# A linear-attention block with an MLP behind it: fewer, wider warming products and a new order of all instructions

## The chip, the cores and the metric

The kernel runs on one core of a Trainium2 chip. The metric is the device time of one execution in microseconds (us); lower is better. The engines are named as in the profile: PE (matrix products), PEld (its weight loads), DVE (vector), ACT (activations), POOL, SP (here it issues all DMAs).

## The reference

For x of 2048 rows and 512 columns (bf16):

```
ln(x)  = (x - mean) / sqrt(var + 1e-5)                  # by row
q,k,v  = split(ln(x) @ wqkv), 32 heads of 16
phi(t) = where(t > 0, t + 1, exp(t)) + 1e-6
kv     = sum_s phi(k)_s v_s^T      z = sum_s phi(k)_s   # by head
o      = (phi(q) kv) / (phi(q) z + 1e-6)
h      = x + o @ wo
out    = h + relu(ln(h) @ w1) @ w2                      # w1: 512 x 1792
```

## The kernel before

Rows come in 16 tiles of 128 (index t) or 4 chunks of 512 (index c). Every instruction is issued by hand: the string ORDER is a list of words such as `K.4.5`, and the last loop of the kernel calls the function of each word in turn. Each engine runs its own instructions in the order of the list, and waits on semaphores where data or a buffer is not ready yet. SP too runs its DMAs in order, and a DMA may not go out before the eighth DMA ahead of it has landed. The numbers behind a word are the tile or chunk, and often the bank of PSUM (0 to 7, the tile `bk`) that the products go to.

The words that the text speaks of, with the engine and the line of the profile before:

- `warm` (PE, L245): products of zeros with zeros, read by nobody, at the very start.
- `lx` (SP, L214), `lk`, `lq`, `lv`, `lo`, `l1`, `l2` (SP, L220): loads of x, of the three parts of wqkv, of wo, w1, w2.
- `S`, `A` (DVE, L248, L249), `R` (ACT, L254 and L255), `N` (DVE, L262): statistics, mean and variance, 1/sqrt, and the normalized tile, which is written to h_nat.
- `T` (PE, L287) and `E` (ACT, L297): the first five tiles are transposed by PE into lnT. `X` (SP, L308): the other eleven are transposed by DMA. `t`, `v`, `x` do the same for the second layer norm (`s`, `a`, `r`, `n`).
- `K` (PE, L316) and `Q` (PE, L324): products for k by tile and for q by chunk, four products of 512 columns each. `F`, `U` (ACT, L334, L337), `M`, `D` (DVE, L341, L344), and `qF` to `qD` for q: phi of them.
- `G` (PE, L368): sums phi(k)^T ln(x) over all tiles in four banks; `kv` (PE, L414) and `m` (PE, L426) bring wv and wo into one matrix m_sb. `z` (PE, L392) sums phi(k).
- `d4` (PE, L440), `dl4`, `dx4` (ACT, L446, L451): the denominators and, by logarithm and exponential, their inverse. `wb` (SP, L468) writes it to memory, eight `rb` (SP, L471) read it back spread over 16 rows each into rr, and `dm` (DVE, L484) multiplies.
- `h` (PE, L493), `hD` (DVE, L499): the attention output plus x.
- `p`, `ph` (PE, L508, L517), `pD`, `pA` (DVE, L528, ACT, L523): ln(h) @ w1 and relu. `f` (PE, L537), `fo` (DVE, L545), `fd` (SP, L552): product with w2, scale and add, and the store of a tile of the output. `f` goes in two halves of seven products.

The word of the warming is read as `warm.<count>.<bank>.<columns>`. A bank is shared by whoever comes next: a product that starts in it waits until the engine that read the last result is done.

Of the kernel before, what the change touches and what calls it, by code (L numbers as in the profile page):

```python
# [15 lines left out]


ORDER = """
table const masks warm.70.7.64 warm.2.7 lx.0.1 S.0 A.0 R.0.1 lx.1.1 S.1 lx.2.1 A.1 N.0 T.0.1 lk.0.4 S.2 R.1.1
N.1 T.1.2 lx.3.1 A.2 E.0 K.0.4 R.2.1 lx.4.2 S.3 N.2 T.2.1 E.1 A.3 S.5 R.3.1 K.1.0.0.2 K.1.0.2.2 N.3 S.4 A.5 A.4  # L20
E.2 T.3.2 K.2.6.0.2 K.2.6.2.2 F.0.1 M.0.1 lx.6.2 E.3 S.7 lq.0.4 R.4.2 lx.8.4 Q.0.3.1 N.4 U.0.1 A.7 F.1.1 F.2.1
T.4.2 N.5 S.6 Q.0.1.4 U.1.1 M.1.1 A.6 lx.12.4 M.2.1 D.0.1 R.6.2 K.3.7.0.2 K.3.7.2.2 E.4 X.5 U.2.1 U.3.1 D.1.1
N.6 Q.0.0.3 N.7 S.10 qF.0.0.2 K.4.5 K.5.6 S.8 A.10 S.9 A.8 qU.0.0.2 S.12 F.4.2 D.2.1 X.6 Q.0.2.0 A.9 A.12 K.6.2
S.13 S.11 M.4.2 A.11 A.13 U.4.2 D.4.2 F.3.1 R.8.2 N.9 M.3.1 X.7 K.7.3 R.12.2 R.10.2 N.8 F.6.2 D.3.1 N.13 S.15
G.0 G.1 U.6.2 S.14 X.9 X.8 N.10 A.14 A.15 N.12 qM.0.0.2 M.6.2 X.13 qF.0.2.2 R.14.2 qU.0.2.2 qM.0.2.2 N.11 G.2
G.3 G.5 G.4 N.14 X.12 K.9.3 K.8.2 K.13.1 N.15 qD.0.0.2 D.6.2 za.4.1 X.11 X.10 F.8.2 U.8.2 M.8.2 K.12.0 U.12.2
F.12.2 G.7 za.6.0 K.11.3 D.8.2 qD.0.2.2 M.12.2 za.8.0 K.10.2 F.10.2 X.14 G.8 K.14.0 U.10.2 X.15 K.15.1 M.10.2 zf
lv.2.2 lv.0.2 G.9 D.10.2 zhi D.12.2 F.14.2 G.6 G.10 G.11 M.14.2 zlo U.14.2 D.14.2 z.0.0 z.2.0 z.3.0 z.1.0 G.14
lo.0.2 lo.2.2 zc zh d4.0.1 dl4.0 l1.0.2 G.13 G.12 G.15 dx4.0 gA.2.2 Q.1.1.3 Q.1.0.2 qF.1.0.2 gD.0.2 kv.1.4
kv.3.4 kv.0.4 kv.2.4 kx qU.1.0.2 qM.1.0.2 qD.1.0.2 Q.1.3.1 Q.1.2.0 qF.1.2.2 m.0.2 m.1.3 mD.0.2 m.3.7 m.2.6 wb.0  # L30
Q.2.0.4 Q.2.1.5 rb.0.7 rb.0.1 rb.0.6 rb.0.3 rb.0.0 rb.0.2 rb.0.4 rb.0.5 l1.2.2 qM.1.2.2 qU.1.2.2 Q.2.3.1
qD.1.2.2 mA.2.2 qF.2.0.2 Q.2.2.0 qU.2.0.2 dm.0.2.2 dm.0.0.2 qM.2.0.2 h.1.6 hD.1 s.1 a.1 qU.2.2.2 d4.1.3 dl4.1
h.0.7 hD.0 s.0 dx4.1 h.2.6 h.3.5 a.0 l2.0.7 wb.1 hD.2 nA.1 hD.3 qF.2.2.2 nA.0 s.2 s.3 Q.3.0.2 Q.3.1.3 a.2
Q.3.3.6 a.3 qF.3.0.2 qU.3.0.2 Q.3.2.5 x.1 r.0.4 qF.3.2.2 n.2 t.2.7 n.3 t.3.4 qD.2.0.2 v.2 v.3 x.0 ph.0.3.1.0
ph.0.1.3.0 ph.0.2.0.0 ph.0.3.1.1 qM.2.2.2 qM.3.0.2 ph.0.0.2.0 ph.0.0.2.1 qM.3.2.2 qD.3.0.2 qU.3.2.2 qD.2.2.2
ph.0.2.0.1 qD.3.2.2 p.0.7.5 d4.2.6.2 pD.0.2.2 dl4.2 dl4.3 rb.1.4 rb.1.6 rb.1.3 rb.1.2 rb.1.0 rb.1.1 ph.0.1.3.1
rb.1.7 rb.1.5 p.0.6.4 dx4.2 dm.1.0.2 dm.1.2.2 h.4.0 pD.0.0.2 hD.4 pD.0.6.2 p.0.5.1 h.6.6 dx4.3 p.0.4.0 hD.6
l2.7.7 h.5.4 pA.0.4.2 s.4 s.6 hD.5 h.7.7 a.4 a.6 p.0.11.6 p.0.10.5 s.5 hD.7 a.5 p.0.9.4 wb.2 rb.2.6 n.4 rb.2.0
rb.2.4 s.7 n.6 rb.2.3 rb.2.2 rb.2.1 a.7 n.5 n.7 rb.2.5 rb.2.7 dm.2.0.2 dm.2.2.2 pD.0.10.2 p.0.13.1 p.0.12.0
p.0.8.3 pD.0.12.2 wb.3 r.4.4 rb.3.0 rb.3.4 h.10.7 hD.10 x.6 h.8.2 h.11.6 hD.8 s.10 rb.3.5 rb.3.1 rb.3.6  # L40
f.1.0.0.7 rb.3.3 rb.3.2 rb.3.7 s.8 hD.11 pD.0.8.2 h.9.5 f.3.1.0.7 x.7 x.5 s.11 a.8 hD.9 f.1.0.7.7 f.0.4.0.7 a.10
a.11 x.4 dm.3.2.2 dm.3.0.2 h.14.7 h.12.3 s.9 n.11 h.15.6 a.9 n.10 h.13.2 fo.1 n.9 n.8 hD.14 s.14 hD.12 x.11
hD.15 f.0.4.7.7 r.8.4 p.1.13.7 p.1.6.3 a.14 hD.13 s.12 s.15 s.13 a.12 a.15 a.13 n.14 p.1.12.6 n.13 f.3.1.7.7
n.12 n.15 p.1.2.5 fo.0 pD.1.12.2 x.10 p.1.7.4 fo.3 p.1.3.6 x.9 pD.1.6.2 pD.1.2.2 r.12.4 x.8 p.1.11.2 p.1.10.1
pD.1.10.2 f.2.4.0.7 p.2.0.6 p.2.1.7 f.2.4.7.7 pD.2.0.2 p.2.10.0 p.2.11.1 fo.2 x.14 p.2.6.2 p.2.7.3 x.15 fd.3
p.2.13.7 p.2.12.6 pD.2.10.2 pD.2.6.2 x.12 fd.1 pD.2.12.2 p.2.2.0 x.13 fd.0 p.2.3.1 p.1.5.6 p.1.4.5 pD.2.2.2
pD.1.4.2 p.1.0.3 p.1.1.4 p.1.9.1 p.1.8.0 pD.1.0.2 pD.1.8.2 f.4.4.0.7 f.4.4.7.7 fo.4 fd.4 f.5.3.0.7 f.5.3.7.7
fo.5 fd.2 f.6.7.0.7 f.6.7.7.7 fo.6 p.2.4.2 p.2.5.3 f.7.0.0.7 f.7.0.7.7 pD.2.4.2 fo.7 p.3.6.1 p.3.7.2 pD.3.6.2
p.3.8.3 p.3.9.4 p.3.5.1 pD.3.8.2 p.3.4.0 pD.3.4.2 fd.6 p.3.10.3 p.3.11.4 pD.3.10.2 p.3.2.0 p.3.3.1 p.3.0.5
p.3.1.6 pD.3.2.2 pD.3.0.2 p.3.13.3 fd.7 p.3.12.2 pD.3.12.2 f.10.1.0.7 f.15.2.0.14.3.1 f.15.7.0.14.0.2 p.2.8.4  # L50
p.2.9.5 fo.15.3.1 fd.15.3.1 fo.15.0.2 pD.2.8.2 f.8.7.0.7 f.10.1.7.7 fo.10 f.8.7.7.7 fo.8 f.14.2.0.7 f.14.2.7.7
f.13.3.0.7 fd.5 fd.8 fd.10 fo.14 f.13.3.7.7 fo.13 f.9.0.0.7 f.9.0.7.7 fd.15.0.2 f.11.6.0.7 f.11.6.7.7 fd.13 fo.9
f.12.0.0.7 fd.9 f.12.0.7.7 fo.11 fd.14 fd.11 fo.12 fd.12 f.15.2.0.14.2.1 fo.15.2.1 fd.15.2.1
"""


# [1 line left out]
def kernel(  # L58
# [14 lines left out]
    S, D = xf.shape  # L73
# [7 lines left out]
    KD = D // P  # L81
    KF = FF // P
# [5 lines left out]
    const = ctx.enter_context(tc.tile_pool(name="const", bufs=1))  # L88
# [58 lines left out]
    rb = big.tile([P, NE, 2, CW], BF16, name="rb")  # L147
# [10 lines left out]
    def pk(t, n=1):  # L158
        return pk_lo[:, t : t + n, :] if t < 2 else acts[0][:, t - 2 : t - 2 + n, :]
# [152 lines left out]
    def op_K(t, b, k=0, n=KD):  # L312
        c, j = divmod(t, CT)
        at_bank["k", t] = b
        for kd in range(k, k + n):
            nc.tensor.matmul(  # L316
                bk[:, b, :], lhsT=lnT[c][:, kd, j * P : (j + 1) * P], rhs=wk_sb[:, kd, :],
                start=(kd == 0), stop=(kd == KD - 1),
            )

    def op_Q(c, j, b):
# [211 lines left out]
    def op_f(t, b, f0, n, k=0, w=KD):  # L533
        c, j = divmod(t, CT)
        at_bank["f", t, k] = b
        for f in range(f0, f0 + n):
            nc.tensor.matmul(  # L537
                bk[:, b, 0 : w * P], lhsT=acts[c % 2][:, f, j * P : (j + 1) * P],
                rhs=w2_sb[:, f, k * P : (k + w) * P],
                start=(f == 0), stop=(f == KF - 1),  # L540
            )

    def op_fo(t, k=0, w=KD):
# [44 lines left out]
```

## Time and profile before

| what | value |
|---|---|
| median of 3 runs | 169.89 us (169.71 to 170.19) |
| span of the profiled execution | 168.0 us |
| between the span and the median | 1.9 us |
| PE busy | 162.7 us (97%) |
| DVE, ACT busy | 115.6 us (69%), 49.5 us (29%) |
| granted TensorE clock, mean | 1.000 |
| DMA | 16.01 MB, 25003 packets |

The span runs from the first to the last instruction of one profiled execution; the time of a run is longer by what lies around it, and no time of the profiled execution apart from its span is given. A row of the timeline begins with the start and the length in us, and "x4" says how many instructions are merged in it. The bracket at its end is the idle time of the engine ahead of it and what ended that. Rows of groups end with busy time, mean length in ns, and idle time before. In the DMA rows the last number is the median time from issue to landing.

### The profile page before, as it was taken

The page shows a single profiled execution, that of the slowest core. Times are in us where ns is not written, and L with a number is a line of the kernel's source. Part 1 is how long each engine was busy: PE and PEld are TensorE (multiplying, and loading weights), DVE is VectorE, ACT ScalarE, POOL GpSimd, SP SyncE. Part 2 cuts the span into 40 slices and gives each one's busy share as a digit, 9 for nine tenths or more (in the row PEclk, how much of TensorE's full clock was granted, in tenths as well). Part 3 has the DMA queues.
Part 4 walks back from the last instruction along what each step waited for, and adds up shares of the span by engine and source line. Part 5 has one row for each costly group of instructions (what it writes and reads, how often), then busy time and mean ns, then how long its engine had stood idle before and what let it go on. Part 6 is the DMA issues. An engine that isn't in the chain of part 4 may idle for free.

```text
span 168.0 us, 2417 instructions
## 1 busy us (share of the span) xinstructions
PE 162.7 (97%) x924; PEld 79.2 (47%) x924; DVE 115.6 (69%) x217; ACT 49.5 (29%) x83; POOL 4.8 (3%) x21
## 2 busy tenths in 40 slices
PE   7799999999999999999999999999999999999992
PEld 7444444454544754444444444444444447444442
DVE  3899999942579999999999755764144773432312
ACT  3799968715798843100101000000000000000000
POOL 7400000000000000000000000000000000000000
PEclk9999999999999999999999999999999999999999
DMA  4984054681595364414552520000101000011021
GB/s 108 353 298 88 20 106 95 189 301 45 132 337 161 98 205 132 132 48 123 83 102 57 126 63 0 0 0 0 62 31 35 0 0 7 32 34 48 31 94 39
DMA packets 25003, 16.01 MB, mean 95 GB/s; under 512 B 15008, under 2 KB 23968, under 8 KB 24992
## 3 DMA queue, kind: packets, MB, share of 16 engines
q1 hardware_dynamic: 24992, 15.87, 33.2%
q8 instruction: 7, 0.11, 0.3%
q14 instruction: 4, 0.03, 0.1%
HBM read 9.96 MB, written 2.62 MB: 75 GB/s over the span
## 4 chain that ended last, share of the span: by engine, by line
PE 92%; DMA 4%; SPq 2%; DVE 1%; issue 0%
PE bk L537 28%; PE bk L508 27%; PE bk L324 8%; PE bk L368 8%; PE bk L493 8%; PE bk L316 7%; DMA wq_sb<-in_A_wqkv_dram 4%; PE bk L517 2%; SPq L214 2%; PE bk L440 1%; DVE gT L545 1%; PE bk L392 1%; PE bk L414 1%; PE bk L426 1%; PE bk L287 0%
## 5 line engine op out<-in xcount | busy, mean ns | idle before, releaser
L537 PE MATMUL bk<-w_sb,at 128*128 128x512 bf16 (+2 forms) x252 | 50.0, 355 | 0.0
L508 PE MATMUL bk<-lnT,w_sb 128*128 128x512 bf16 x208 | 46.9, 379 | 0.0
L528 DVE TENSOR_SCALAR at<-bk 128x1024 bf16<-128x1024 f32 x27 | 32.8, 1223 | 13.2 <-PE bk L508 13.2
L537 PEld LDWEIGHTS <-at 128*128 128x128 bf16 x252 | 23.5, 98 | 25.4
L508 PEld LDWEIGHTS <-w_sb 128*128 128x128 bf16 x208 | 20.4, 98 | 23.9
L545 DVE SCALAR_TENSOR_TENSOR gT<-bk,rstd,h_nat 128x512 bf16<-128x512 f32 (+2 forms) x18 | 12.4, 691 | 24.6 <-PE bk L537 22.0
L334 ACT ACTIVATE eb<-bk 128x1024 bf16<-128x1024 f32 (+1 forms) x18 | 16.6, 929 | 5.3 <-PE bk L316 2.8
L337 ACT ACTIVATE rb<-bk 128x1024 bf16<-128x1024 f32 (+1 forms) x18 | 16.4, 929 | 0.0
L324 PE MATMUL bk<-lnT,wq_sb 128*128 128x512 bf16 x64 | 15.1, 379 | 0.3 <-DMA wq_sb<-in_A_wqkv_dram 0.3
L316 PE MATMUL bk<-wk_sb,lnT 128*128 128x512 bf16 x64 | 15.3, 379 | 0.0
L493 PE MATMUL bk<-m_sb,pqs 128*128 128x512 bf16 x64 | 15.1, 379 | 0.0
L368 PE MATMUL bk<-at,h_nat 128*128 128x512 bf16 x56 | 13.1, 379 | 0.0
L248 DVE BATCH_NORM_STATS2 st<-x_nat 128x6 f32<-128x512 bf16 x16 | 10.6, 678 | 2.3 <-DMA x_nat<-in_A_x_dram 2.3
L499 DVE TENSOR_TENSOR h_nat<-bk,x_nat 128x512 bf16<-128x512 f32 x16 | 10.6, 676 | 0.9 <-PE bk L493 0.9
L254 ACT ACTIVATE rstd<-mv,eps 128x2 f32<-128x2 f32 (+2 forms) x14 | 4.2, 297 | 23.7 <-DVE mv L251 20.9
L250 DVE BATCH_NORM_STATS2 st<-h_nat 128x6 f32<-128x512 bf16 x16 | 10.5, 684 | 0.1
L324 PEld LDWEIGHTS <-wq_sb 128*128 128x128 bf16 x64 | 6.1, 98 | 7.7 <-DMA wq_sb<-in_A_wqkv_dram 0.8
L493 PEld LDWEIGHTS <-pqs 128*128 128x128 bf16 x64 | 6.1, 98 | 7.7 <-DVE pqs L484 0.6
L368 PEld LDWEIGHTS <-h_nat 128*128 128x128 bf16 x64 | 6.1, 98 | 7.3 <-issue 0.2
L316 PEld LDWEIGHTS <-lnT 128*128 128x128 bf16 x64 | 6.1, 98 | 6.8
L341 DVE TENSOR_SCALAR eb<-eb 128x1024 bf16<-128x1024 bf16 (+1 forms) x18 | 6.6, 389 | 0.0
L262 DVE TENSOR_SCALAR h_nat<-x_nat,mv,rstd 128x512 bf16<-128x512 bf16 x16 | 6.3, 408 | 0.2 <-ACT rstd L255 0.2
(65 smaller groups left out, 87.7 us busy)
## 6 DMA issues: line engine op xcount, KB each, us to landing
w_sb<-in_B_w_dram SPq DMA_DIRECT2D x4, 896.0 KB, 6.2
rr<-scr SPq DMA_DIRECT2D x32, 64.0 KB, 2.6
out_dram<-gT SPq DMA_DIRECT2D x15, 128.0 KB, 1.9
x_nat<-in_A_x_dram SPq DMA_DIRECT2D x2, 512.0 KB, 7.9
x_nat<-in_A_x_dram SPq DMA_DIRECT2D x4, 128.0 KB, 2.2
wk_sb<-in_A_wqkv_dram SPq DMA_DIRECT2D x1, 512.0 KB, 4.1
x_nat<-in_A_x_dram SPq DMA_DIRECT2D x2, 256.0 KB, 4.6
wq_sb<-in_A_wqkv_dram SPq DMA_DIRECT2D x1, 512.0 KB, 6.2
```

The lines of the kernel that those rows point to most:

```text
L248: op_S = lambda t: nc.vector.bn_stats(out=st[:, t, :], in_=x_nat[:, t, :])
L316: nc.tensor.matmul(bk[:, b, :], lhsT=lnT[c][:, kd, j * P : (j + 1) * P], rhs=wk_sb[:, kd, :], start=(kd == 0), stop=(kd == KD - 1),)
L324: nc.tensor.matmul(bk[:, b, :], lhsT=wq_sb[:, kd, j * P : (j + 1) * P], rhs=lnT[c][:, kd, :], start=(kd == 0), stop=(kd == KD - 1),)
L334: nc.scalar.activation(out=buf(eb, kind, i, n), in_=bank(at_bank[kind, i], n), func=ACT.Exp)
L337: nc.scalar.activation(out=buf(rb, kind, i, n), in_=bank(at_bank[kind, i], n), func=ACT.Relu)
L368: nc.tensor.matmul(bk[:, KD + kd, :], lhsT=ln_nat[:, t, kd * P : (kd + 1) * P], rhs=pk(t)[:, 0, :], start=(not stated), stop=(len(stated) ...
L493: nc.tensor.matmul(bk[:, b, :], lhsT=pqs[:, (c * KD + jb) % NQ, j * P : (j + 1) * P], rhs=m_sb[:, jb, :], start=(jb == 0), stop=(jb == KD ...
L499: nc.vector.tensor_tensor(out=h_nat[:, t : t + n, :], in0=bank(at_bank["h", t], n), in1=x_nat[:, t : t + n, :], op=ALU.add,)
L508: nc.tensor.matmul(bk[:, b, :], lhsT=w1_sb[:, kd, f * P : (f + 1) * P], rhs=lnT[c][:, kd, :], start=(kd == 0), stop=(kd == KD - 1),)
L528: nc.vector.tensor_scalar(out=acts[c % 2][:, f : f + n, :], in0=bank(at_bank["p", c, f], n), scalar1=-1.0, scalar2=0.0, op0=ALU.mult, op1= ...
L537: nc.tensor.matmul(bk[:, b, 0 : w * P], lhsT=acts[c % 2][:, f, j * P : (j + 1) * P], rhs=w2_sb[:, f, k * P : (k + w) * P], start=(f == 0), ...
L545: nc.vector.scalar_tensor_tensor(out=o_t[:, t % NO, cols], in0=bk[:, at_bank["f", t, k], 0 : w * P], scalar=rstd2[:, t : t + 1], in1=h_nat ...
```

## The change

The warming is 35 products of 128 columns in place of 70 of 64; two products of 512 columns follow in both. The whole list ORDER is written anew. Words are the same in kind and number otherwise, and so are the tiles that are transposed by PE, the halves and the buffers; what differs is their order on each engine and the bank that a word names. Two products' start and stop flags are now set by counting the calls for the same sum, so that halves of a K or of an f may be issued in either order.

```diff
 ORDER = """
-table const masks warm.70.7.64 warm.2.7 lx.0.1 S.0 A.0 R.0.1 lx.1.1 S.1 lx.2.1 A.1 N.0 T.0.1 lk.0.4 S.2 R.1.1
-N.1 T.1.2 lx.3.1 A.2 E.0 K.0.4 R.2.1 lx.4.2 S.3 N.2 T.2.1 E.1 A.3 S.5 R.3.1 K.1.0.0.2 K.1.0.2.2 N.3 S.4 A.5 A.4
-E.2 T.3.2 K.2.6.0.2 K.2.6.2.2 F.0.1 M.0.1 lx.6.2 E.3 S.7 lq.0.4 R.4.2 lx.8.4 Q.0.3.1 N.4 U.0.1 A.7 F.1.1 F.2.1
-T.4.2 N.5 S.6 Q.0.1.4 U.1.1 M.1.1 A.6 lx.12.4 M.2.1 D.0.1 R.6.2 K.3.7.0.2 K.3.7.2.2 E.4 X.5 U.2.1 U.3.1 D.1.1
-N.6 Q.0.0.3 N.7 S.10 qF.0.0.2 K.4.5 K.5.6 S.8 A.10 S.9 A.8 qU.0.0.2 S.12 F.4.2 D.2.1 X.6 Q.0.2.0 A.9 A.12 K.6.2
...
+table const lx.0.1 warm.35.7.128 lx.1.1 masks lx.2.1 lk.0.4 lx.3.1 S.0 lx.4.2 S.1 lx.6.2 lq.0.4 A.0 A.1 warm.2.7
+S.2 R.0.1 lx.8.4 R.1.1 N.0 lx.12.4 A.2 N.1 T.0.2 R.2.1 T.1.4 E.0 N.2 E.1 T.2.1 S.3 K.0.6 E.2 A.3 S.4 K.1.0.0.2
+R.3.1 K.1.0.2.2 F.0.1 N.3 A.4 U.0.1 S.5 T.3.5 K.2.2.2.2 E.3 S.7 K.2.2.0.2 U.1.1 K.3.7.2.2 A.5 M.0.1 R.4.2 S.6
+K.3.7.0.2 F.1.1 Q.0.1.4 A.7 A.6 N.4 F.3.1 N.5 R.6.2 T.4.5 M.1.1 X.5 D.0.1 Q.0.0.3 F.2.1 M.3.1 D.1.1 E.4 N.6
+Q.0.2.0 U.2.1 S.9 X.6 qF.0.0.2 K.4.5 N.7 S.11 X.7 qU.0.0.2 K.5.6 A.9 S.13 S.8 Q.0.3.1 U.3.1 F.4.2 S.12 K.6.2
+qM.0.0.2 U.4.2 A.8 D.3.1 K.7.3 S.10 R.8.2 M.4.2 G.3 F.6.2 M.2.1 N.8 D.2.1 X.8 G.0 A.12 N.9 A.13 S.14 R.12.2 G.1
+U.6.2 X.9 D.4.2 G.2 N.13 qF.0.2.2 S.15 X.13 G.4 A.11 A.10 N.12 R.10.2 A.15 A.14 K.8.2 M.6.2 qU.0.2.2 lv.2.2 N.11
+D.6.2 X.12 K.9.3 R.14.2 qM.0.2.2 qD.0.0.2 K.13.1 X.11 N.15 F.8.2 N.14 G.6 N.10 za.4.1 U.8.2 X.10 G.7 qD.0.2.2
+K.12.0 X.14 M.8.2 G.5 za.6.0 F.12.2 X.15 K.10.2 U.12.2 D.8.2 K.11.3 za.8.0 l1.0.2 lv.0.2 K.14.0 U.10.2 lo.0.2
+M.12.2 l2.0.7 zf K.15.1 F.10.2 D.12.2 G.9 F.14.2 M.10.2 G.13 D.10.2 U.14.2 zhi G.8 M.14.2 zlo Q.1.1.3 D.14.2 z.1.2
+z.0.2 z.2.2 z.3.2 G.14 zc zh d4.0.0 G.12 dl4.0 dx4.0 G.15 wb.0 G.11 lo.2.2 G.10 rb.0.3 Q.1.0.2 gA.2.2 gD.0.2
+rb.0.4 Q.1.2.0 rb.0.2 qU.1.0.2 rb.0.0 kv.2.7 rb.0.1 kv.3.7 qF.1.0.2 kv.1.7 rb.0.6 kv.0.7 Q.1.3.1 rb.0.7 kx rb.0.5
+qM.1.0.2 Q.2.1.5 qF.1.2.2 l1.2.2 qD.1.0.2 m.1.4 m.0.3 qU.1.2.2 m.3.2 mD.0.2 Q.2.2.6 m.2.1 Q.2.3.7 qM.1.2.2 mA.2.2
+dm.0.0.2 Q.2.0.4 dm.0.2.2 qF.2.2.2 qD.1.2.2 h.1.1 qF.2.0.2 qM.2.2.2 h.0.0 hD.1 qU.2.0.2 h.3.2 s.1 a.1 hD.0 h.2.1
...
+qD.3.0.2 rb.1.1 p.0.11.4 pD.0.0.2 rb.1.4 ph.0.3.3.1 rb.1.5 qD.2.2.2 ph.0.2.2.1 l2.7.7 p.0.12.5 pD.0.2.2 d4.2.6.2
+p.0.7.1 dl4.3 dm.1.2.2 dl4.2 p.0.5.7 dx4.3 p.0.10.3 dx4.2 r.0.4 wb.2 p.0.8.2 pD.0.10.2 wb.3 p.0.4.6 dm.1.0.2
...
+f.13.1.7.7 f.11.6.7.7 fo.13 f.15.2.0.14.3.1 f.12.1.0.7 fo.15.3.1 fd.15.3.1 fd.13 f.9.3.0.7 f.9.3.7.7 f.11.6.0.7
+fo.9 fo.15.0.2 fd.15.0.2 f.14.5.7.7 f.14.5.0.7 fo.11 fd.11 f.12.1.7.7 fo.14 fd.14 fd.9 f.15.7.0.14.2.1 fo.12 fd.12
+fo.15.2.1 fd.15.2.1
 """
@@
+    fed = {}
+
+    def part(key, n):
+        at = fed[key] = fed.get(key, 0) + 1
+        return {"start": at == 1, "stop": at == n}
+
@@ op_K
-                start=(kd == 0), stop=(kd == KD - 1),
+                **part(("k", t), KD),
@@ op_f
-                start=(f == 0), stop=(f == KF - 1),
+                **part(("f", t, k), KF),
```

The words of before around the places that the prediction names: `za.8.0 K.10.2 F.10.2 X.14 G.8 K.14.0 U.10.2 X.15 K.15.1 M.10.2 zf lv.2.2 lv.0.2 G.9` for the loads behind the transposes, `lo.0.2 lo.2.2 zc zh d4.0.1 dl4.0 l1.0.2`, `m.2.6 wb.0 Q.2.0.4 Q.2.1.5 rb.0.7 rb.0.1`, and at the end `f.12.0.7.7 fo.11 fd.14 fd.11 fo.12 fd.12 f.15.2.0.14.2.1 fo.15.2.1 fd.15.2.1`.

More of the change, by code (lines that the diff above doesn't have):

```diff
@@ L24 @@
[L24 to L53, printed above, removed]
+table const lx.0.1 warm.35.7.128 lx.1.1 masks lx.2.1 lk.0.4 lx.3.1 S.0 lx.4.2 S.1 lx.6.2 lq.0.4 A.0 A.1 warm.2.7
@@ new lines @@
+rb.0.4 Q.1.2.0 rb.0.2 qU.1.0.2 rb.0.0 kv.2.7 rb.0.1 kv.3.7 qF.1.0.2 kv.1.7 rb.0.6 kv.0.7 Q.1.3.1 rb.0.7 kx rb.0.5
+qM.1.0.2 Q.2.1.5 qF.1.2.2 l1.2.2 qD.1.0.2 m.1.4 m.0.3 qU.1.2.2 m.3.2 mD.0.2 Q.2.2.6 m.2.1 Q.2.3.7 qM.1.2.2 mA.2.2
+dm.0.0.2 Q.2.0.4 dm.0.2.2 qF.2.2.2 qD.1.2.2 h.1.1 qF.2.0.2 qM.2.2.2 h.0.0 hD.1 qU.2.0.2 h.3.2 s.1 a.1 hD.0 h.2.1
+nA.1 s.0 x.1 Q.3.1.5 a.0 hD.3 nA.0 Q.3.2.0 hD.2 qU.2.2.2 x.0 d4.1.3 s.3 Q.3.3.1 dl4.1 s.2 Q.3.0.4 dx4.1 a.2 a.3
+n.2 qF.3.2.2 n.3 wb.1 t.2.6 t.3.2 v.2 ph.0.1.7.0 qF.3.0.2 v.3 ph.0.3.3.0 qM.2.0.2 ph.0.1.7.1 qU.3.2.2 qD.2.0.2
@@ new lines @@
+rb.1.3 ph.0.0.6.1 rb.1.0 qM.3.2.2 ph.0.0.6.0 qU.3.0.2 qM.3.0.2 rb.1.2 ph.0.2.2.0 qD.3.2.2 rb.1.7 p.0.6.0 rb.1.6
+qD.3.0.2 rb.1.1 p.0.11.4 pD.0.0.2 rb.1.4 ph.0.3.3.1 rb.1.5 qD.2.2.2 ph.0.2.2.1 l2.7.7 p.0.12.5 pD.0.2.2 d4.2.6.2
+p.0.7.1 dl4.3 dm.1.2.2 dl4.2 p.0.5.7 dx4.3 p.0.10.3 dx4.2 r.0.4 wb.2 p.0.8.2 pD.0.10.2 wb.3 p.0.4.6 dm.1.0.2
+p.0.9.3 pA.0.4.2 pD.0.6.2 rb.2.4 rb.2.7 h.4.4 rb.2.0 pD.0.8.2 rb.2.6 p.0.13.6 rb.2.5 f.2.1.0.7 rb.2.1 pD.0.12.2
+rb.2.3 rb.2.2 hD.4 f.0.5.7.7 s.4 h.5.3 h.7.4 hD.5 f.2.1.7.7 hD.7 dm.2.2.2 s.7 h.6.2 dm.2.0.2 f.3.6.0.7 s.5 rb.3.3
@@ new lines @@
+rb.3.5 a.4 a.7 a.5 n.7 rb.3.4 hD.6 h.10.0 x.7 s.6 f.3.6.7.7 n.5 fo.2 rb.3.7 rb.3.0 a.6 n.4 r.4.4 h.8.2 rb.3.6 fo.3
+rb.3.1 hD.10 h.9.4 rb.3.2 x.4 hD.8 f.1.7.0.7 hD.9 fd.3 x.5 f.1.7.7.7 dm.3.0.2 n.6 dm.3.2.2 x.6 h.11.0 h.12.4 hD.11
+s.8 h.14.2 s.11 f.0.5.0.7 hD.14 s.9 fo.1 p.1.9.2 a.8 s.10 p.1.1.7 a.11 n.8 n.11 p.1.2.0 x.8 a.10 n.10 a.9 fo.0
+r.8.4 p.1.8.1 s.14 h.13.3 n.9 hD.12 x.9 h.15.5 hD.13 p.1.7.4 x.10 hD.15 a.14 p.1.0.6 pD.1.8.2 fd.2 p.1.6.3 fd.0
+pD.1.0.2 x.11 p.1.13.5 pD.1.6.2 p.1.4.2 p.1.3.1 p.2.7.7 pD.1.2.2 p.1.5.3 p.2.6.6 pD.1.4.2 f.7.1.0.7 pD.2.6.2
@@ new lines @@
+p.1.12.4 s.13 a.13 p.2.11.7 n.14 s.15 p.2.2.2 pD.1.12.2 p.2.3.3 n.13 p.1.10.5 pD.2.2.2 p.1.11.6 s.12 p.2.4.2 a.15
+pD.1.10.2 p.2.5.3 f.4.5.0.7 pD.2.4.2 f.6.0.7.7 p.2.10.6 f.6.0.0.7 p.2.1.3 fo.6 pD.2.10.2 p.2.0.2 fd.6 f.7.1.7.7
+n.15 a.12 x.15 n.12 r.12.4 p.2.13.4 fo.7 x.12 pD.2.0.2 f.4.5.7.7 x.14 p.2.12.3 fd.1 p.2.8.1 x.13 pD.2.12.2
+f.5.0.7.7 p.2.9.2 p.3.8.3 pD.2.8.2 p.3.9.4 p.3.7.7 pD.3.8.2 f.5.0.0.7 fo.4 p.3.3.1 fo.5 p.3.10.5 fd.5 p.3.6.6
+f.10.2.0.7 pD.3.6.2 f.10.2.7.7 p.3.2.0 p.3.12.3 pD.3.2.2 p.3.11.6 fo.10 p.3.13.4 pD.3.10.2 fd.10 fd.7 p.3.5.2 fd.4
@@ L54 @@
+p.3.4.1 p.3.1.7 pD.3.4.2 f.8.0.7.7 p.3.0.6 f.8.0.0.7 pD.3.0.2 pD.3.12.2 f.13.1.0.7 fo.8 f.15.4.0.14.0.2 fd.8
+f.13.1.7.7 f.11.6.7.7 fo.13 f.15.2.0.14.3.1 f.12.1.0.7 fo.15.3.1 fd.15.3.1 fd.13 f.9.3.0.7 f.9.3.7.7 f.11.6.0.7
+fo.9 fo.15.0.2 fd.15.0.2 f.14.5.7.7 f.14.5.0.7 fo.11 fd.11 f.12.1.7.7 fo.14 fd.14 fd.9 f.15.7.0.14.2.1 fo.12 fd.12
+fo.15.2.1 fd.15.2.1
 """
```

## The prediction

> **What bounds the kernel now.** I read the windows of busy time first, then PE's own timeline of the first microseconds.
>
> ```profile
> 5.00:10.38 5.38, 4.12 (x30) 1.83 (x29) 4.85 (x15) 4.41 (x14) 1.05 (x4) 1.00 1.07 381
> 10.38:165.00 154.62, 154.59 (x824) 73.74 (x824) 108.16 (x193) 43.09 (x67) 0.00 (x0) 1.00 0.31 85
> 165.00:168.00 3.00, 0.00 (x0) 0.00 (x0) 0.35 (x1) 0.00 (x0) 0.00 (x0) 1.00 0.18 55
> ```
>
> After the stretch and its length the first number is PE's busy time. From 10.38 to 165 PE idles 0.03 us of 154.62. So no later wait is there to be removed: a new order can win ahead of 10.38, where PE is busy 4.12 of 5.38 us, or in the 3.0 us behind 165, and it can lose anywhere.
>
> ```profile
> 1.05 4.08 PE L245 MATMUL bk<-m_sb 128*128 128x64 bf16 x72 [1.05 <-DVE m_sb L186]
> 5.09 0.40 PE L287 MATMUL bk<-ident,h_nat 128*128 128x128 bf16 x4
> 6.08 0.40 PE L287 MATMUL bk<-ident,h_nat 128*128 128x128 bf16 x4 [0.59 <-DVE h_nat L262]
> 6.32 1.03 PE L316 MATMUL bk<-wk_sb,lnT 128*128 128x512 bf16 x4
> 7.68 0.40 PE L287 MATMUL bk<-ident,h_nat 128*128 128x128 bf16 x4 [0.34 <-DVE h_nat L262]
> 7.92 1.03 PE L316 MATMUL bk<-wk_sb,lnT 128*128 128x512 bf16 x4
> 8.79 0.40 PE L287 MATMUL bk<-ident,h_nat 128*128 128x128 bf16 x4
> 9.02 1.03 PE L316 MATMUL bk<-wk_sb,lnT 128*128 128x512 bf16 x4
> 10.38 1.04 PE L324 MATMUL bk<-lnT,wq_sb 128*128 128x512 bf16 x4 [0.33 <-DMA wq_sb<-in_A_wqkv_dram]
> ```
>
> These are the warming, T.0, T.1, K.0, T.2, K.1, T.3, K.2 and the first Q, which stood waiting for wq (landed about 10.33). A row's length holds the drain of its last product; in a packed stretch a group of four products of 512 columns costs PE 0.86, and a transposed tile 0.23 (8.79 to 9.02). Three rows of the chain of waits, for the 0.86 and for later (kv, the first h, a pair of d4):
>
> ```profile
> 42.42 0.89 PE bk L414 x16
> ...
> 49.36 0.86 PE bk L493 x4
> ...
> 61.07 0.55 PE bk L440 x8
> ```
>
> The profiled execution spans 168.0; the median of three runs is 169.89, so 1.9 us lie around the span, and I carry them over.
>
> **Warming.** 70 products of 64 columns become 35 of 128: 4480 columns in both, and the two of 512 stay. If time goes by columns, the 4.08 us stay; if by products, they end some 2 us earlier. Neither reaches the end, since the first real product of the new order starts at 5.5, behind both (below): nothing. All other products are the same in number and shape.
>
> **The head: the gain.** SP issues its first ten loads in the same order, so I keep their landings. What changes is what DVE and PE do between them.
>
> ```profile
> 3.98 0.29 ACT L254 ACTIVATE rstd<-mv,eps 128x1 f32<-128x1 f32 x1 [1.90 <-DVE mv L249]
> 4.30 0.20 ACT L255 ACTIVATE rstd<-rstd 128x1 f32<-128x1 f32 x1
> ```
> ```profile
> 3.03 0.69 DVE L248 BATCH_NORM_STATS2 st<-x_nat 128x6 f32<-128x512 bf16 x1 [1.79 <-DMA x_nat<-in_A_x_dram]
> ...
> 6.62 0.69 DVE L248 BATCH_NORM_STATS2 st<-x_nat 128x6 f32<-128x512 bf16 x1 [0.51 <-DMA x_nat<-in_A_x_dram]
> ...
> 8.32 0.41 DVE L262 TENSOR_SCALAR h_nat<-x_nat,mv,rstd 128x512 bf16<-128x512 bf16 x1
> 8.64 0.69 DVE L248 BATCH_NORM_STATS2 st<-x_nat 128x6 f32<-128x512 bf16 x1
> 9.25 0.30 DVE L249 BATCH_NORM_AGGREGATE mv<-st 128x2 f32<-128x6 f32 x2
> ```
>
> An S holds DVE for 0.61 (8.64 to 9.25), and two A take 0.30. DVE now does S.0 and S.1 (3.03 to 4.3), A.0 and A.1 (to 4.55), S.2 (to 5.1); ACT does R.0 beside S.2 (0.29 + 0.20, to 5.0). N.0 (0.41) ends at 5.5: T.0 at 5.53, not 5.09. N.1 follows at once (T.1 at 5.94); A.2, R.2 and N.2 put T.2 at 6.66. K.0 runs from 6.88, K.1 from 7.75 to 8.61. S.3 still waits for its tile until 6.62; A.3, R.3 and N.3 end near 8.6, and T.3 meets PE with almost no idle time at 8.62. K.2 (8.85) covers the copy of T.3's result, K.3 follows at 9.71, the first Q at 10.57, behind wq's landing, and ends at 11.43. Before, at 11.24 (10.38 + 0.86) PE had done four transposes, three K and one Q, and K.3 was still to cost 0.86: 12.10. So **0.67 us gained**, T.0's lateness of 0.44 included: K.3 now fills the wait for wq.
>
> **The transposes by DMA: given back.** Behind 11.43 PE does T.4 (0.23), Q.0.0, Q.0.2, K.4 and is at K.5 at 14.25. K.5 reads what X.5 writes, and X.5 goes out behind N.5. Counted from S.3 at 6.62, N.2 is gone from DVE (0.41) and S.6 and A.6 come in (0.7): X.5 at 11.4 to 11.6, against 11.10 before.
>
> ```profile
> q8 instruction: 1, 0.02, 4.5%
> ...
> lnT<-h_nat SPq DMA_TRANSPOSE x1, 3.4
> ```
> ```profile
> q8 instruction: 7, 0.11, 0.3%
> ...
> lnT<-h_nat SPq DMA_TRANSPOSE x11, 2.4
> ```
> ```profile
> 19.41 10.37 SPq L308 DMA_TRANSPOSE lnT<-h_nat  x8
> ```
>
> The first fence is the DMA view of 11 to 12.5 us alone, the second that of the whole execution. The first transpose took 3.4 us to land where the median is 2.4, and beside it ran one instruction fetch, which held one of the 16 engines for 1.1 us (4.5% x 16 x 1.5). With 2.4 X.5 lands by 14.0 and K.5 doesn't wait; with 3.4 at 14.9, and K.5 waits about 0.7. I take the former, since the fetch moves away: it came when PE had run 72 + 30 + 5 products, each with its weight load; without 35 warming ones PE gets there 35 real products later, near 18 us.
>
> On this the Trainium skill has a rule (Runtime: NRT & Kernel Launch, Instruction fetch mechanics): engines fetch instructions in 16 KiB blocks ahead of need, at a cost that is mostly hidden. By that rule the fetch is no reason for the 3.4 us; it belongs to the first transpose and comes again.
>
> The second train starts with X.8. Eight in a row took 10.37; with 1.2 for the last one alone they go out every 1.3 us. N.8 stands behind four A and one D fewer, and one qM and one M more, than N.9 did, which started this train before: X.8 goes out at 18.6 to 19.1 instead of 19.41. X.10 is the sixth of the train, with one load of wv (0.6 us on SP) now put between: 18.6 + 5 x 1.3 + 0.6 + 2.4 = 28.1, or 28.6. PE reaches K.10 sixteen groups after K.5, at 14.25 + 13.8 = 28.07. A wait of 0 to 0.5; I take 0.2, nearer the early end. If K.5 had to wait, this one shrinks by as much.
>
> **The denominators: given back.** p.0.5.7 takes the bank of the second d4 group, with only p.0.7.1 between them.
>
> ```profile
> L440 PE MATMUL bk<-pqT,zhd 128*32 128x512 bf16 x16 | 1.4, 387 | 0.0
> ```
> ```profile
> L446 ACT ACTIVATE ld<-bk,eps 128x512 f32<-128x512 f32 x4 | 2.6, 686 | 6.0 <-PE bk L440 6.0
> ```
>
> The eight d4 products hold PE for 0.55; the last starts about 0.5 after the first and takes 0.39, then the logarithm dl4.3 takes 0.69. With two hand-overs of 0.03 (3.98 + 0.29 to 4.30 on ACT is one) the bank is free after 1.64. PE is there after 0.55 + 0.86 = 1.41: **0.23 lost**, whatever happened before.
>
> **Loads and the end.** The loads of w1, w2, wv and wo change places on SP's queue.
>
> ```profile
> w_sb<-in_B_w_dram SPq DMA_DIRECT2D x4, 896.0 KB, 6.2
> rr<-scr SPq DMA_DIRECT2D x32, 64.0 KB, 2.6
> ```
> ```profile
> 39.43 0.34 SPq L468 DMA_DIRECT2D scr<-rd  x1
> 41.17 3.62 SPq L471 DMA_DIRECT2D rr<-scr  x8
> ```
>
> Those that now go out near 30, right behind the transposes, have 12 us until kv at 42.4, twice the 6.2 of the largest: nothing. One wo (256 KB) now goes between wb.0 and the eight rb.0: nothing if rr lands in time (rival 1). The last two groups of products and fo.12, fd.12, fo.15, fd.15 stand as before, so the 3.0 us stay. For other places where a release meets PE within 0.1 us I add 0.15, between nothing (PE has no idle time there to win) and 0.4 (four such places).
>
> **The sum.** -0.67 + 0 + 0.2 + 0.23 + 0.15 = -0.09: span 167.9, time 169.8. That is no change: 0.3% is 0.5 us, about what a measurement of this kernel can tell from none.
>
> **The rivals.** (1) *Slower: rr comes late.* Before, wb.0 went out at 39.43 and the eight rb from 41.17, the last near 44.4; it landed near 47.0, 7.5 us behind wb.0. In the new order wb.0 is out near 38.9, rr would be in at 46.4, and with wo's 256 KB ahead (0.7 us at 381 GB/s) at 47.1; dm takes 0.7, and PE is at h.1 near 48.5. 0.7 to spare. If the train is later by 1.4 us PE waits 0.7: 170.5. It decides above 0.7, and DVE's queue makes it worse, since hD, s and a stand behind dm. Against it: before, h.1 (49.36) did not wait. (2) *The first transpose takes 3.4 again*, as by the page's rule: K.5 waits 0.7 and the second train's 0.2 is gone: 170.3. For it: its kind is new at that point, whatever runs beside it. (3) *Faster*: the tight places hold (second train and allowance at nothing): -0.67 + 0.23 = -0.44; and where wq lands later than in the profile, before pays and after is covered for 0.24: 169.3. For it: PE's wait for wq is the last before a packed stretch, so each 0.1 there was 0.1 of time. (4) *The head does half of what it says*: N.3 late by 0.3, with R.3 behind other work on ACT: 170.1.
>
> **How the numbers follow.** Forecast (169.8) 0.36, rival 1 and other late buffers like it 0.22, rival 2 0.16 (half of it above 170.4), rival 3 0.18, rival 4 0.08. Faster by over 0.3%: 0.18. Slower: 0.22 + 0.08, and 0.02 where others meet: 0.32. Within: 0.50. The range takes in rivals 3 and 1 and the bounds of the unknown costs: from -0.67 (169.2) to -0.09 + 0.7 + 0.25 (170.75).
>
> **What would show it.** T.0 near 5.5, the first Q near 10.6 without a wait for wq, K.5 near 14.25; one wait of PE for dl4.3 near 64; no instruction packet beside the first transpose, and that one in 2.4 us. Wrong would be: PE waits of over 0.6 us in sum behind 11.4, above all for lnT or pqs; a first Q behind 11; an end other than 3.0 us behind the last product.

## The result and the profile after

| kernel | median | runs | ratio to before, 95% interval | span of the profiled execution |
|---|---|---|---|---|
| before | 169.78 us (169.34 to 170.19) | 14 | | 168.0 us |
| after | 170.89 us (170.02 to 171.85) | 14 | 1.0065 (1.0045 to 1.0085) | 169.2 us |

The change makes the kernel 0.65% slower. The forecast was no change, 169.8; the time is 0.14 us above the top of its range (170.75). I read the profile after in the order of before: the windows first (after the stretch and its length, PE's busy time), then PE's timeline, the waits, and the chain of waits around the two stretches that stand out.

```profile
5.00:10.66 5.66, 5.47 (x34) 2.58 (x34) 5.08 (x15) 5.19 (x16) 1.10 (x4) 1.00 1.06 381
10.66:16.10 5.44, 5.44 (x29) 2.47 (x27) 5.44 (x17) 5.41 (x11) 0.00 (x0) 1.00 0.59 96
16.10:20.00 3.90, 2.74 (x13) 1.26 (x14) 3.90 (x14) 2.64 (x5) 0.00 (x0) 1.00 0.24 46
20.00:80.00 60.00, 59.62 (x352) 29.37 (x357) 46.59 (x87) 32.64 (x45) 0.00 (x0) 1.00 0.47 136
80.00:90.00 10.00, 9.69 (x45) 4.16 (x45) 7.73 (x16) 0.50 (x2) 0.00 (x0) 1.00 0.49 115
90.00:166.18 76.18, 75.81 (x374) 35.89 (x379) 44.41 (x64) 1.00 (x4) 0.00 (x0) 1.00 0.14 37
166.18:169.20 3.02, 0.00 (x0) 0.00 (x0) 0.36 (x2) 0.00 (x0) 0.00 (x0) 1.00 0.26 83
```

The end is the 3.0 us of before. One stretch is bad: PE idles 1.16 of the 3.90 us from 16.1 to 20, where before had no idle time.

```profile
1.05 4.77 PE L251 MATMUL bk<-m_sb 128*128 128x128 bf16 x37 [1.05 <-DVE m_sb L192]
5.61 1.31 PE L293 MATMUL bk<-ident,h_nat 128*128 128x128 bf16 x12
...
10.66 1.03 PE L330 MATMUL bk<-lnT,wq_sb 128*128 128x512 bf16 x4
...
15.20 1.03 PE L330 MATMUL bk<-lnT,wq_sb 128*128 128x512 bf16 x4
17.33 0.82 PE L322 MATMUL bk<-wk_sb,lnT 128*128 128x512 bf16 x3 [1.10 <-DMA lnT<-h_nat]
```

The lines of after stand 6 below those of before (L322 is K, L330 is Q, L314 is X, L315 is x, L499 is h). The first Q starts at 10.66 and waits for no wq. K.6 could start at 15.20 + 0.86 = 16.06; it starts at 17.33, so it costs 1.27 us. The waits of PE and of its weight loads (us in total, times, longest):

```profile
PEld L322 <- DMA lnT<-h_nat: 2.0, 3, 1.6
...
PEld L499 <- DVE pqs L490: 1.1, 2, 0.7
```

The chain of waits at K.6, and the row of the first train on SP's queue (min, median and max in ns of the time that issuing takes, then in us of issue to landing):

```profile
13.02 4.26 DMA lnT<-h_nat
17.28 0.05 issue
17.33 0.82 PE bk L322 x3
```
```profile
L314 SPq DMA_TRANSPOSE lnT<-h_nat x3: 1191/1281/2449, 11.6 to 14.3; - x3
...
DMA to landing us min/median/max: 2.6/3.7/4.3
```

X.6 took 4.26 us to land in place of some 2.5, and X.7's issue behind it 2.45 in place of 1.2. X.5, the first transpose by DMA of this execution, landed in 2.6. What ran beside X.6 is in the DMA view of 14.15 to 15.75 (by queue: packets, MB, share of 16 engines; then issues, KB each, us to landing):

```profile
q8 instruction: 1, 0.02, 5.9%
...
lnT<-h_nat SPq DMA_TRANSPOSE x2, 4.0
```

One instruction packet of 16 KB, which held one of the 16 engines for 5.9% x 16 x 1.6 = 1.5 us. In before the packet lay beside X.5 (the 3.4 us of the prediction), which landed at 14.5 and was needed at 14.9; here it lies beside the transpose that PE needs next.

The second place is h.12. The chain of waits there comes first. In the DMA view of 78 to 84 us, below it, another such packet (the fourth, at 80.3) lies beside x.7 and the last eight rb:

```profile
80.17 2.24 SPq L315
82.41 0.04 issue
...
87.27 0.69 DVE pqs L490
...
88.88 1.25 PE bk L499 x5
```
```profile
q8 instruction: 1, 0.02, 1.1%
...
lnT<-hn SPq DMA_TRANSPOSE x1, 3.4
```

x.7 held SP for 2.24 us (1.21 with the old warming, below), the five rb behind it went out 1 us later, dm waited 2.2 us for rr (1.1 with the old warming), and h.12 for dm: PE idles 0.31 us between 80 and 90, and by the starts of its products, which show the wait in front of each, it loses 0.44. With -0.58 in the head (below), +1.27 at K.6, +0.44 at h.12 and some 0.1 in small pieces elsewhere, the sum is +1.2: 168.0 to 169.2.

### The profile page after: what moved, and what is told of

The parts are those of the page before. It is cut to its first block, busy times and chain, and to the rows that moved or that the text cites. A ratio compares the mean times of both kernels' runs of the same rounds, so it can differ in the third digit from the quotient of the medians.

```text
span 169.2 us, 2325 instructions
## 1 busy us (share of the span) xinstructions
PE 162.7 (96%) x873; PEld 79.6 (47%) x889; DVE 115.9 (69%) x217; ACT 49.3 (29%) x83; POOL 4.8 (3%) x21
## 4 chain that ended last, share of the span: by engine, by line
PE 82%; DVE 6%; SPq 3%; DMA 3%; issue 2%; ACT 1%; DVEq 0%
PE bk L514 27%; PE bk L543 23%; PE bk L374 8%; PE bk L330 6%; PE bk L499 5%; PE bk L322 5%; PE bk L251 3%; DMA lnT<-h_nat 3%; PE bk L523 2%; SPq L477 2%; DVE pqs L490 2%; SPq L315 1%; DVE st L254 1%; ACT lnT L303 1%; DVE h_nat L268 1%
## 5 line engine op out<-in xcount | busy, mean ns | idle before, releaser
L543 PE MATMUL bk<-w_sb,at 128*128 128x512 bf16 (+2 forms) x247 | 50.6, 355 | 0.2
L322 PE MATMUL bk<-wk_sb,lnT 128*128 128x512 bf16 x62 | 14.9, 379 | 1.2 <-DMA lnT<-h_nat 1.1
L499 PE MATMUL bk<-m_sb,pqs 128*128 128x512 bf16 x63 | 15.3, 379 | 0.3 <-DVE pqs L490 0.3
L330 PE MATMUL bk<-lnT,wq_sb 128*128 128x512 bf16 x62 | 15.4, 379 | 0.1
L322 PEld LDWEIGHTS <-lnT 128*128 128x128 bf16 x64 | 6.0, 98 | 8.6 <-DMA lnT<-h_nat 2.0
L499 PEld LDWEIGHTS <-pqs 128*128 128x128 bf16 x64 | 6.1, 98 | 8.2 <-DVE pqs L490 1.1
L330 PEld LDWEIGHTS <-wq_sb 128*128 128x128 bf16 x64 | 6.1, 98 | 7.1 <-issue 0.2
L490 DVE TENSOR_TENSOR pqs<-pqT,rr 128x1024 bf16<-128x1024 bf16 x8 | 5.4, 685 | 3.0 <-DMA rr<-scr 3.0
```

Of the source, the lines that this page charges most:

```text
L322: nc.tensor.matmul(bk[:, b, :], lhsT=lnT[c][:, kd, j * P : (j + 1) * P], rhs=wk_sb[:, kd, :], **part(("k", t), KD),)
L330: nc.tensor.matmul(bk[:, b, :], lhsT=wq_sb[:, kd, j * P : (j + 1) * P], rhs=lnT[c][:, kd, :], start=(kd == 0), stop=(kd == KD - 1),)
L499: nc.tensor.matmul(bk[:, b, :], lhsT=pqs[:, (c * KD + jb) % NQ, j * P : (j + 1) * P], rhs=m_sb[:, jb, :], start=(jb == 0), stop=(jb == KD ...
L543: nc.tensor.matmul(bk[:, b, 0 : w * P], lhsT=acts[c % 2][:, f, j * P : (j + 1) * P], rhs=w2_sb[:, f, k * P : (k + w) * P], **part(("f", t, ...
```

## The experiments

Theory F: the 16 KB packet of PE's instruction fetch holds up the transposes and reads in flight when it comes; fewer warming products move the packet, and so decide what it meets. Theory O: the new order is too tight whatever is fetched. Theory W, added later: fewer, wider warming products cost by themselves. Each kernel but the repeat of after changes the words of the warming alone, and keeps its 4480 (or 4472) columns.

**The new order with the old warming.**

```diff
-table const lx.0.1 warm.35.7.128 lx.1.1
+table const lx.0.1 warm.70.7.64 lx.1.1
```

> The order of after with the warming of before (70 products of 64 columns). Theory F (the instruction fetch of PE beside X.6 is what made it late): 35 more products, each with its weight load, ahead of the work bring the first fetch forward to 8 to 11.5 us; X.6 lands in 2.4 to 2.5 us instead of 4.3, K.6 does not wait (1.27 us less idle), X.5 may take 3.4 and K.5 wait up to 0.7; the fetch that stood at 80.3 comes near 72 and h.12 waits 0.1 or less. Time 169.3 to 170.0. Theory O (the new order itself leaves the transposes too little room, the fetch only happened to be there): K.6 waits about 1.3 again, time 170.6 to 171.1.

Measured: 169.49 us (12 runs), ratio to before 0.9988 (0.9969 to 1.0007), span 167.6. The first train of this kernel, and the DMA view of 12.9 to 17.5:

```profile
L314 SPq DMA_TRANSPOSE lnT<-h_nat x3: 1192/1217/1282, 11.7 to 14.4; - x3
...
DMA to landing us min/median/max: 2.4/2.5/2.6
```
```profile
q1 hardware_dynamic: 1634, 0.40, 42.9%
```

There is no instruction packet in this stretch (it comes at 10.9), no late transpose, and no wait at K.6 or h.12. The order itself costs nothing that can be measured.

**The old order with the new warming.**

```diff
-table const masks warm.70.7.64 warm.2.7 lx.0.1
+table const masks warm.35.7.128 warm.2.7 lx.0.1
```

> The order of before with the warming of after (35 products of 128 columns). Theory F: the first fetch leaves 11.4 us and comes between 14 and 18 us; X.5 lands in 2.4 us instead of 3.4; if the fetch meets X.6 or X.7, K.6 or K.7 waits 0.5 to 1.0 and the time is 170.2 to 170.8, if it comes behind 17 us nothing waits: 169.7. Theory O: no wait anywhere, since this order starts K.6 0.6 us later than after does: 169.6 to 169.9, wherever the fetch comes.

Measured: 171.11 us (6 runs), 1.0069 (1.0042 to 1.0097), span 169.3. The chain of waits at K.6, and the DMA view of 14.4 to 16.1:

```profile
13.48 4.15 DMA lnT<-h_nat
17.63 0.04 issue
17.68 1.47 PE bk L316 x6
```
```profile
q8 instruction: 1, 0.02, 6.0%
```

The warming alone brings the whole loss, with the same transpose and a wait of 1.2 us; the time is above what F had put down. O falls, since it allowed no wait in this order. The fourth packet, at 81.6, makes x.5 and x.4 late too (4.4 and 3.9 us to land), and PE does not wait for them.

**The new order with 18 warming products.**

```diff
-table const lx.0.1 warm.35.7.128 lx.1.1
+table const lx.0.1 warm.17.7.256 warm.1.7.128 lx.1.1
```

> The order of after with 17 warming products of 256 columns and one of 128: the same 4480 columns in 17 instructions pairs fewer. Theory F: the first fetch comes at 18 to 22 us, X.6 lands in 2.4 to 2.5, K.6 does not wait; the fetch meets X.8 or X.9 instead, and one of K.9, K.13, K.10 waits 0 to 1.0. The fetch of 80.3 comes near 83, so rr of chunk 3 and h.12 stay late by about 0.4. Time 169.6 to 170.6. Theory O: K.6 waits 1.3 again, time 170.6 to 171.1.

Measured: 170.40 us (12 runs), 1.0043 (1.0022 to 1.0064), span 168.6. The packet comes at 18.0, between the landing of X.7 (17.05) and the issue of X.8 (18.86), and K.6 does not wait. What is left is mostly h.12: the fourth packet comes at 81.2, on x.7 and the last rb, and the weight loads wait for pqs. By the starts of its products PE loses 0.6 us there; the other 0.2 against the old warming are lost ahead of the first Q, which starts at 10.95 in place of 10.74.

```profile
PEld L499 <- DVE pqs L490: 1.3, 2, 0.8
```

**After once more**, one execution, to see whether place and size come again.

> The changed kernel once more, for a second profile. Theory F: the first 16 KB instruction packet starts between 13.5 and 15 us, X.6 lands over 3.5 us after its issue, K.6 waits over 0.8 us. Theory O: K.6 waits about 1.3 whatever the fetch's time is. If the runs of 170.0 are those in which the fetch misses X.6, a time below 170.3 comes with no wait at K.6.

Measured: 170.94 us, span 169.2. The packet came at 14.7, X.6 took 4.18 us, K.6 waited 1.2. A packet at 80.9 cost h.12 less than 0.1: that term varies between executions. So does the head. S.3 waits for its load of x until 7.29 (6.51 in the first execution), T.3 comes 0.57 later and so does the first Q:

```profile
7.29 0.69 DVE L254 BATCH_NORM_STATS2 st<-x_nat 128x6 f32<-128x512 bf16 x1 [0.57 <-DMA x_nat<-in_A_x_dram]
```
```profile
9.27 0.40 PE L293 MATMUL bk<-ident,h_nat 128*128 128x128 bf16 x4 [0.36 <-DVE h_nat L268]
...
11.23 1.03 PE L330 MATMUL bk<-lnT,wq_sb 128*128 128x512 bf16 x4
```

The span is the same by other parts: nothing from the head, and nearly nothing lost at h.12.

**The old order with 18 warming products.** F says that going further in the direction that made it slower makes it faster again.

```diff
-table const masks warm.70.7.64 warm.2.7 lx.0.1
+table const masks warm.17.7.256 warm.1.7.128 warm.2.7 lx.0.1
```

> The order of before, its 70 warming products of 64 columns replaced by 17 of 256 and one of 128 (the same 4480 columns). Theory F (the 16 KB packet of PE's instruction fetch holds up the transposes in flight): the first packet comes near 18 us, as in the new order with the same warming (17.99), behind the first train (X.5 to X.7 landed by 17) and ahead of X.8 at 19.4; so the loss that 35 products cause in this order (1.22 us ahead of K.6) is gone again: X.6 lands in 2.4 to 2.6 us, PE waits under 0.2 us for it, and the time is 169.7 to 170.4, the upper part if the packet near 81 us falls on a train again. Rival W (fewer and wider warming products are themselves what costs, by the clock or by PE's pipeline): the loss grows with every step away from 70: 171.1 or more.

Measured: 170.14 us (12 runs), 1.0019 (0.9998 to 1.004), span 168.3. The first train and the DMA view of 11 to 18 us:

```profile
L308 SPq DMA_TRANSPOSE lnT<-h_nat x3: 1193/1217/1288, 11.3 to 14.7; - x3
...
DMA to landing us min/median/max: 2.4/2.5/2.6
```
```profile
q1 hardware_dynamic: 1682, 0.54, 33.2%
...
lnT<-h_nat SPq DMA_TRANSPOSE x3, 2.5
```

The packet comes at 18.3, between the trains, and most of the loss is gone (1.0019 in place of 1.0069). W, which wanted a larger loss, falls as the cause.

**The new order with 26 warming products.** F has to move the wait to another transpose.

```diff
-table const lx.0.1 warm.35.7.128 lx.1.1
+table const lx.0.1 warm.26.7.172 lx.1.1
```

> The new order with 26 warming products of 172 columns (4472 columns), between 35 (packet at 14.2, 170.9) and 18 (packet at 18.0, 170.4). Theory F: the packet comes near 16, while X.7 (out at 14.9, due at 17.4) is in flight: X.7 lands late by 0.8 to 1.8 us, near 18.2 to 19. K.7 starts behind K.6 and Q.0.3, at 18: a wait of 0.2 to 1.0 us at K.7 and none at K.6; with the packet near 81 us on the last rr train as in both neighbours, 170.3 to 171.2. Rival W: between its neighbours, 170.4 to 170.9, with the wait where it was or with none.

Measured: 171.16 us (6 runs), 1.0089 (1.0058 to 1.0121), span 169.3. The chain of waits, and the DMA view of 15.5 to 17.2:

```profile
14.60 3.98 DMA lnT<-h_nat
18.58 0.05 issue
18.63 1.04 PE bk L322 x4
```
```profile
q8 instruction: 1, 0.02, 5.7%
...
lnT<-h_nat SPq DMA_TRANSPOSE x1, 4.0
```

The packet is at 15.6, X.7 is the one that takes 3.98 us, K.7 waits (1.4 us, more than the 0.2 to 1.0 of F), and K.6 does not.

**The new order with 9 warming products.**

```diff
-table const lx.0.1 warm.35.7.128 lx.1.1
+table const lx.0.1 warm.8.7.512 warm.1.7.384 lx.1.1
```

> The new order with warming of 8 products of 512 columns and one of 384 (the same 4480 columns). Theory F: the first packet comes when 8 to 9 more real products have run than with 18 warming products, 1.7 to 2 us later, at 19.6 to 20, on the second train: X.8 or X.9 lands in 3.5 to 4.3 us in place of 2.5, and the transposes behind it go out 1 us later; PE waits 0.5 to 1.2 us in sum at K.8, K.9 or K.13, and the time is 170.5 to 171.3. Rival W: slower than with 18 products too (170.4), 170.6 to 171.5, but then without a wait that follows a packet. A packet that hits nothing: 170.2 to 170.5.

Measured: 170.16 us (12 runs), 1.0013 (0.9987 to 1.0039), span 168.8. The packet came at 19.6 and X.8 took 3.7 us, as F has it, but PE needed X.8 late: the transposes cost PE some 0.3 us, not 0.5 to 1.2, and the time is below F's range (one of the twelve runs took 217.3 us). The fourth packet is at 84.2, when the last rb is out, and h.12 does not wait. Its first Q starts at 11.62, nearly 1 us behind after's: PE waits for T.3 (S.3's load is late here too) and for wq. The place was right and the price wrong: a late transpose costs only what goes beyond its slack.

**The new order with 52 warming products**, twice, since the profiled execution of the first ran 608 us, with PE busy for 596 of them.

```diff
-table const lx.0.1 warm.35.7.128 lx.1.1
+table const lx.0.1 warm.52.7.86 lx.1.1
```

> The new order with 52 warming products of 86 columns (4472 columns). Theory F: the first packet comes between those of 70 products (10.9) and of 35 (14.2), near 12 to 13, while X.5 (out at 11.7) is in flight: X.5 lands 0.7 to 1.8 us late, near 15 to 16; PE is at K.5 at 15, so it waits 0 to 0.9 us there, and the time is 169.6 to 170.5. Rival W: halfway between 70 products and 35, 170.1 to 170.3, without a packet beside the wait.

> The new order with 52 warming products of 86 columns once more (171.09 in the run before; in the execution that was profiled every product took four times as long, so that trace says nothing on the loss). Theory F has to show a packet on a transpose that PE needs at once: between 12.5 and 14 us, X.5 or X.6 landing in 3.4 to 4.3 us, and a wait of 0.8 to 1.5 us at K.5 or K.6; 170.7 to 171.3. Rival W2 (the width of 86 columns, or a start of the packed stretch that varies, costs by itself): a later first product, or products longer than 0.216 us in a packed stretch, and no such wait.

Measured: 171.09 us (8 runs with the one of 609.8 us; 170.86 over the other seven), 1.0073 (1.0043 to 1.0103); then 170.62 us (12 runs), 1.0053 (1.0028 to 1.0077), span 168.9, just below what I had put down. The first packet came at 11.4, 0.5 us ahead of X.5's issue, and X.5 landed in 2.6: the wait that I had put at K.5 or K.6 is not there. W2 falls too: T.0 starts at 5.61, as in after, and the products of a packed stretch stand 0.216 us apart. The loss is at another place, with the third packet (55.8). The chain of waits there, and the DMA view of 55.7 to 56.9:

```profile
53.96 3.88 DMA lnT<-hn
57.84 0.05 issue
57.89 1.16 PE bk L523 x9
```
```profile
q8 instruction: 1, 0.02, 5.4%
```

A transpose of the second layer norm is hit, and ph waits 1.1 us for it. So every packet of the kernel counts, not the first alone.

**The new order with the old warming again**, for the interval.

> The new order with the warming of before (70 products of 64 columns) once more, for a narrower interval on what the order alone is worth. Theory F: ratio 0.996 to 1.000, the first packet near 10.9, no wait over 0.2 us behind the head. If the 0.3 to 0.4 us that the span showed are real, the ratio is 0.998; if the order itself costs anything, over 1.000.

Measured: 169.58 us (12 runs), 0.9984 (0.9959 to 1.0008), span 167.8. Twice a ratio just under 1, and neither interval leaves 1 out: the order alone is worth at most a few tenths of a us. No run here beats before by what can be measured.

## Why the prediction was wrong, point by point

**The step that failed is "the transposes by DMA: given back", first train.** I put it at 0 "since the fetch moves away", to near 18 us. The fetch did move, but to 14.2, onto X.6, and it cost 1.27 us. The sign that I had named for being wrong, waits of over 0.6 us behind 11.4 for lnT or pqs, is what came. I saw the packet in the profile and its length beside X.5, and read the kind of its effect rightly; its place was wrong, and a hit cost more than the 0.7 that I had put down for one. I let it come when PE had run as many products as in before (72 + 30 + 5 = 107). Counted in the traces, 82 to 88 products had started when it came in each of the runs with 9 to 52 warming products, and 103 to 108 in those with 70. Nineteen products of 0.22 us are the 4 us between 18 and 14.2. Why the count differs with 70 thin ones, which pass in the first 5 us, was not tried. A range of 14 to 18 for the packet would have given the first train a price of 0 to 1.3.

**Warming at "nothing"** left out a product's place in the instruction stream: in the new order, 35 products fewer moved all seven packets. Its length was misjudged too, at almost no cost. The warming did reach T.0, whose weights went in at 5.42 and whose first product starts at 5.61, when the last warming product is over:

```profile
5.42 0.80 PEld L293 LDWEIGHTS <-h_nat 128*128 128x128 bf16 x8 [0.51 <-DVE h_nat L268]
```

In before the last two warming products, of 512 columns, started 0.22 us apart and the warming was over at 4.97; in after they started 0.43 apart, at 4.76 and 5.18. PE ran at that half pace until 4.24 in before and 5.93 in after, and with the same 70 products in the new order until 3.92 in one execution and some 6.9 in the other, so the number of products alone does not set it; what does is not shown. K.0 started at 6.86 in after, as forecast (6.88).

**Rival 2** (a late first transpose again, 0.7 at K.5) had the right kind of wait but not its mechanism. A transpose's first use is not slow: X.5 landed in 2.6 in after, and in 2.6 in each of the other profiles of these experiments, where the packet was elsewhere. The Trainium skill's rule (Runtime: NRT & Kernel Launch, Instruction fetch mechanics), that the fetch of a 16 KiB block is mostly hidden, agrees with the runs with 70 products and with the packet at 18 us, and not with after: PE is not short of instructions there, it waits for X.6, which came late beside the packet, and that is 1.27 us at K.6. That the transpose lacked the DMA engine which the packet held is the likely way, but no view shows it.

**The head** was right for the profiled execution, with some luck: 0.67 predicted. In after the four T, four K and one Q are done at 10.66 + 0.86 = 11.52, in before at 12.10 by the prediction's count: 0.58. T.0 was forecast at 5.53 and started at 5.61. But I had kept the landings of before, and they vary: in other executions of the new order the first Q starts at 10.74 and 10.95 (old warming), 11.23 (after once more) and 11.62 (9 products), which leaves 0.50, 0.29, nothing, and a loss. In the old order it starts at 10.38, 10.21 and 10.13. So rival 4, a head worth half or less, is met as well, ahead of the packet.

**The second train (0.2) and the denominators (0.23)** cost nothing that shows. From 20 to 80 us PE idles 0.38 us in sum, and none of its waits there is for lnT or for the bank of dl4.3:

```profile
63.85 0.61 PE L446 MATMUL bk<-pqT,zhd 128*32 128x512 bf16 x8
64.40 1.90 PE L514 MATMUL bk<-lnT,w_sb 128*128 128x512 bf16 x8
```
```profile
64.52 1.26 ACT L452 ACTIVATE ld<-bk,eps 128x512 f32<-128x512 f32 x2 [3.86 <-PE bk L446]
```

ACT starts dl4.3 at 0.67 behind the first d4, and two of them take 1.26, so the first is done near 0.67 + 0.63 = 1.30; PE is at p.0.5.7 after 1.41. I had put 0.5 + 0.39 + 0.06 + 0.69 = 1.64 there: the eight d4 overlap, and the last is done 0.61 behind the first, not 0.89.

**The allowance of 0.15** stood for late releases by tight buffers. What came was h.12, by a packet: 0.44 in the profiled execution, under 0.1 in another, and 0.6 with 18 warming products.

**Rival 1** (rr late at h.1) did not happen: no wait for pqs ahead of 80 us. **Rival 3** had its condition, since the tight places held, and still not its time: only with the old warming does the kernel come near, at 169.5 and 169.6 (its own sum gives 169.89 - 0.44 - 0.24 = 169.2, not 169.3).

With -0.50 and -0.29 for the head, 0 for both trains, the denominators and rival 1, and some 0.1 in small pieces, the sum is what the new order does with the old warming: spans of 167.6 and 167.8 against 168.0. With -0.58 for the head, 1.27 and 0.44 at the packets it is after.

## What to carry to other kernels

Find the instruction packets in the DMA view before you cost a change in the number of instructions, even of instructions that do no work: each packet here held one DMA engine for 0.9 to 1.6 us, and the transposes in flight beside it landed 0.6 to 2 us late. Ask which transfer lies at each new place and how much slack it has, and give the place a range, since here it followed the number of products (82 to 88 with 9 to 52 of warming) more than the time (11.4 to 19.6 us), and not even that number held with 70. A kernel whose order is laid out without slack behind its DMAs should be timed over a few instruction counts before a loss or a gain is put down to the order.

## What was not expected of the hardware

- A packet of 1.5 us costs a transpose in flight more than its own length: 4.26, 4.18, 4.15 and 3.98 us to land in place of 2.5, and the issue of the next one 2.4 us in place of 1.2 where one followed at once. Why it is 1.5 to 1.8 us, and why the next issue waits, stays open; the traces show only that they go together. They do so without exception: in the eleven traces of 167 to 170 us, all 19 transposes that were issued between 1.9 us ahead of a packet's start and 0.3 us behind it took 3.05 to 4.43 us to land, and the eight that overlapped one otherwise (issued 2.2 us or more ahead, or 0.5 or more behind) took 2.4 to 2.6. Without any packet, beside other transfers, 3.4 was the most.
- The wait follows the packet from transpose to transpose: X.6 (packet at 14.2 to 14.7), X.7 (15.6), X.8 (19.6), a transpose of the second norm (55.8), and there is none in the first train with the packet at 10.9 to 11.4 or 18.0 to 18.3, when no transpose that PE needed soon was in flight.
- With the same 4480 (or 4472) columns of warming the time of the new order went 169.5 (70 products), 170.9 and 170.6 (52, without the run of 609.8), 170.9 (35), 171.2 (26), 170.4 (18), 170.2 (9): not monotonic, over a span of 1.7 us, without one product of the computation changed.
